# The first tiles of a fused retention and gated feed-forward kernel are re-ordered, and two more chunks are transposed by DMA

## The chip, the cores and the metric

The kernel runs on one NeuronCore of one Trainium2 chip. The metric is device time in microseconds, the lower the better. Median before: 242.88 us over nine runs (242.76 to 243.0).

## What is computed

The reference is a retention layer followed by a gated feed-forward layer:

```
gamma[h] = 1 - 2**(-5-h);  scale = 1/sqrt(64)
for t in range(768):                       # for each of 4 batches, 8 heads
    state = gamma*state + outer(k[t], v[t])
    y[t]  = scale * q[t] @ state
x   = y, heads side by side                # 3072 tokens x 512
out = (sigmoid(x @ w_gate) * (x @ w_val)) @ w_out    # 512 -> 1536 -> 512
```

All inputs and the output are float32 in device memory. There are 3072 tokens.

## The kernel before

**Chunks and tiles.** The recurrence is computed in 24 chunks of 128 tokens, six to a batch; chunk `g` is chunk `g % 6` of batch `g // 6`. Four chunks make a token tile of 512, and there are six tiles. Attention for a chunk has these steps, each a small function:

- `transposes` (L134): eight TensorE transposes of k and q, copied from PSUM by ScalarE (L140). For chunks `g >= XBAR` (12), `xbar` (L142) does it with two DMA transposes on SP's queue instead.
- `scale_v` (L148): v times a decay table `tabv`, on VectorE for chunks below 8 and on GpSimd from there on.
- `scores` (L153): eight products k.q into two PSUM banks; `masks` (L162): two VectorE multiplications with the causal mask.
- `inter` (L168): four products of the running state `zbd` with q; `state` (L175): eight products k.v that are added to the state in PSUM; `state_out` (L185): two ScalarE copies of it into `zbd`.
- `intra` (L192): eight products of the masked scores with v; `y_out` (L199): VectorE multiplies the result with a decay table `taby` into `xT`, the feed-forward's input, already transposed.

**Feed-forward.** `up(t, n1)` (L235) makes one of 12 blocks of 128 hidden columns: four matmuls with `wg` and four with `wv` into two PSUM banks, a Sigmoid on ScalarE (L246), a product on VectorE (L247). The pool `pf` has three such banks. `down(t, sm)` (L249) makes 128 of the tile's output rows with twelve matmuls, a ScalarE copy into one of three `ob` buffers (L255) and a store on SP's queue (L257).

**Order.** The schedule is written by hand: each engine runs its instructions in the order of the program. The first three chunks are done before any feed-forward work (L275 to L319), with Identity products (`keep_on`, L259) placed between the steps on TensorE. The fourth chunk is mixed with the first four ups, which take 384 columns at first and 128 more when the fourth chunk is there (L332). From then on, tile `t`'s loop (L336) places the nine attention steps of tile `t + 1` evenly between its 12 ups and 4 downs; in tile 0 they begin after the seventh group.

**Queues.** GpSimd's queue issues nearly all loads, in program order: chunks 1 to 3, weights, chunks 4 to 7; then, when tile `t` begins, the loads of tile `t + 2`'s chunks, and after them the four `scale_v` of tile `t + 1`'s chunks, where these are GpSimd's. So chunk 8's scaling stands behind the loads of chunks 12 to 15. A load on this queue also waits until the load eight places before it has landed, since eight semaphores are used in turn. SP's queue holds the stores and the DMA transposes: those for chunks 12 to 15 stand between tile 0's four stores and tile 1's.

The functions that the diff touches:

Of the kernel before, what the change touches and what calls it, by code (L numbers as in the profile page):

```python
# [17 lines left out]
def kernel(  # L18
# [31 lines left out]

    NG = B * NCH
    NT = N_TOK // 512
    XBAR = 12
    qn, kn, vf = {}, {}, {}

    def src(x, g):
        b, c = divmod(g, NCH)
        return x[b, :, c * C:(c + 1) * C, :].rearrange("h s d -> s h d")
# [11 lines left out]
    def load_chunk(g):  # L70
        load_kq(g)
        load_v(g, nc.gpsimd)
# [16 lines left out]
    kf = const.tile([C, H, D], F32, name="kf")  # L89
    qf = const.tile([C, H, D], F32, name="qf")  # L90
    nc.sync.dma_start(out=kf, in_=src(k, 0))
    nc.scalar.dma_start(out=qf, in_=src(q, 0))
    load_v(0, nc.sync)
    tokv = const.tile([128, NCH], I32, name="tokv")
    nc.gpsimd.iota(tokv, pattern=[[C, NCH]], base=0, channel_multiplier=1)
    ident = const.tile([128, 128], BF16, name="ident")
    make_identity(nc, ident)
    toky = const.tile([128, S], I32, name="toky")
    nc.gpsimd.iota(toky, pattern=[[1, S]], base=0, channel_multiplier=0)
    load_chunk(1)  # L100
    causal = const.tile([128, 128], F32, name="causal")
    nc.gpsimd.memset(causal, 1.0)
# [10 lines left out]
    for p in range(NP):  # L113
        nc.vector.memset(lgp[0:D, p:p + 1], lg[2 * p])
        nc.vector.memset(lgp[D:128, p:p + 1], lg[2 * p + 1])
    zbd = [const.tile([128, NP, C], BF16, name=f"zbd{i}") for i in range(2)]
    for t in zbd:
        nc.vector.memset(t, 0.0)
# [2 lines left out]
    def make_taby(cols):  # L121
        for p in range(NP):
            nc.scalar.activation(taby[:, p, cols], toky[:, cols], AX.Exp, scale=lgp[:, p:p + 1], bias=lsc)  # L123

    causal4 = causal.unsqueeze(1).to_broadcast([128, NP, 128])

# [7 lines left out]
    def transposes(g):  # L134
        tp = pa.tile([128, 2 * NP, C], BF16, tag="tp", name="tp")
        for i, x in enumerate((kn[g], qn[g])):
            for p in range(NP):
                nc.tensor.transpose(tp[:, i * NP + p, :], pair(x, p), ident)  # L138
        qkT[g] = at.tile([128, 2 * NP, C], BF16, tag="qkT", name="qkT", bufs=3)
        nc.scalar.activation(qkT[g], tp, AX.Copy)  # L140
# [7 lines left out]
    def scale_v(g, eng):  # L148
        vs[g] = ld.tile([C, H, D], BF16, tag="vs", name="vs", bufs=4)
        eng.tensor_tensor(vs[g], vf[g], tabv[:, g % NCH, :].unsqueeze(2).to_broadcast([C, H, D]),  # L150
                          op=ALU.mult)

    def scores(g):  # L153
        t = qkT[g]
        sc[g] = (pa.tile([128, NP, C], F32, tag="sA", name="sA"),
                 pa.tile([128, NP, C], F32, tag="sB", name="sB"))
        for p in range(NP):
            for i in range(2):
                half = slice(i * D, (i + 1) * D)
                nc.tensor.matmul(sc[g][i][:, p, :], t[half, p, :], t[half, NP + p, :], start=True, stop=True)  # L160

    def masks(g):  # L162
        stA[g] = at.tile([128, NP, C], BF16, tag="stA", name="stA")
        stB[g] = at.tile([128, NP, C], BF16, tag="stB", name="stB")
        nc.vector.tensor_tensor(stA[g], sc[g][0], causal4, op=ALU.mult)  # L165
        nc.vector.tensor_tensor(stB[g], sc[g][1], causal4, op=ALU.mult)  # L166

    def inter(g):  # L168
        y[g] = pa.tile([128, NP, C], F32, tag="y", name="y")
        if g % NCH > 0:  # L170
            for p in range(NP):
                nc.tensor.matmul(y[g][:, p, :], zbd[(g - 1) % 2][:, p, :], qkT[g][:, NP + p, :],  # L172
                                 start=(p == 0), stop=False, skip_group_check=True)

    def state(g):  # L175
        b, c = divmod(g, NCH)
        if c == 0:
            zps[b] = pa.tile([128, NP, D], F32, tag="z", name="z", padded_shape=[128, NP, C])
        if c < NCH - 1:
            for p in range(NP):  # L180
                for i in range(2):
                    nc.tensor.matmul(zps[b][i * D:(i + 1) * D, p, :], kn[g][:, 2 * p + i, :], vs[g][:, 2 * p + i, :],  # L182
                                     start=(c == 0 and p == 0), stop=True, skip_group_check=True)
# [8 lines left out]
    def intra(g):  # L192
        first = g % NCH == 0
        for p in range(NP):
            for i, st in enumerate((stA[g], stB[g])):
                nc.tensor.matmul(y[g][i * D:(i + 1) * D, p, :], vs[g][:, 2 * p + i, :], st[:, p, :],  # L196
                                 start=(first and p == 0), stop=True, skip_group_check=True)

    def y_out(g):  # L199
        c = g % NCH  # L200
        if g % 4 == 0:
            xT[g // 4] = at.tile([128, NP, 512], BF16, tag="xT", name="xT")
        col = (g % 4) * C
        nc.vector.tensor_tensor(xT[g // 4][:, :, col:col + C], y[g], taby[:, :, c * C:(c + 1) * C], op=ALU.mult)  # L204
# [21 lines left out]
    def attention(t):  # L226
        g = 4 * t
        return [lambda: step_t(g), lambda: step_s(g), lambda: step_t(g + 1), lambda: step_y(g, g + 1),
                lambda: step_t(g + 2), lambda: step_y(g + 1, g + 2), lambda: step_t(g + 3),
                lambda: step_y(g + 2, g + 3), lambda: step_y(g + 3)]  # L230
# [39 lines left out]
    for s in range(4):  # L270
        load_out(s)
    for g in range(5, 8):
        load_chunk(g)

    kn[0] = ld.tile([C, H, D], BF16, tag="kn", name="kn")  # L275
    qn[0] = ld.tile([C, H, D], BF16, tag="qn", name="qn")
    make_taby(slice(0, 256))
    nc.vector.tensor_copy(kn[0], kf)
    nc.scalar.copy(qn[0], qf)
    keep_on(36)  # L280
    transposes(0)
    keep_on(8)
    scale_v(0, nc.vector)
    scores(0)
    state(0)
    state_out(0)
    masks(0)
    keep_on(8)
    make_taby(slice(256, 384))
    transposes(1)  # L290
    scale_v(1, nc.vector)
    inter(0)
    intra(0)
    y_out(0)
    keep_on(10)
    scores(1)
    state(1)
    state_out(1)
    masks(1)
    inter(1)  # L300
    keep_on(10)
    make_taby(slice(384, 512))
    transposes(2)
    intra(1)
    scale_v(2, nc.vector)
    y_out(1)
    keep_on(12)
    scores(2)
    state(2)
    state_out(2)  # L310
    masks(2)
    inter(2)
    keep_on(12)
    make_taby(slice(512, 768))
    nc.scalar.preload_act_table(AX.Sigmoid)  # L315
    intra(2)
    y_out(2)
    scale_v(3, nc.vector)
    keep_on(8)  # L319
    up(0, 0, 0, 384)  # L320
    transposes(3)
    up(0, 1, 0, 384)
    scores(3)
    masks(3)
    inter(3)
# [3 lines left out]
    intra(3)  # L329
    y_out(3)  # L330
    up(0, 3, 0, 384)
    for n1 in range(4):  # L332
        up(0, n1, 384, 512)


    for t in range(NT):  # L336
        groups = [lambda n1=n1: up(t, n1) for n1 in range(0 if t else 4, NFF)]
        groups += [lambda sm=sm: down(t, sm) for sm in range(4)]
        steps = attention(t + 1) if t + 1 < NT else []
        if t + 2 < NT:  # L340
            for g in range(4 * t + 8, 4 * t + 12):
                load_chunk(g)
        first = 0 if t else 6
        done = 0
        for i, group in enumerate(groups):
            if i == len(groups) - 5:
                for g in range(4 * t + 8, 4 * t + 12):
                    if XBAR <= g < NG:
                        xbar(g)
            group()  # L350
            upto = -(-len(steps) * (i + 1 - first) // (len(groups) - first))
            while done < min(upto, len(steps)):
                steps[done]()
                done += 1


# [28 lines left out]
```

## Time and profile before

| | |
|---|---|
| median of nine runs | 242.88 us |
| the profiled execution: device time | 242.81 us |
| its span, first to last instruction | 241.1 us |
| granted TensorE clock | 1.000 |
| TensorE busy | 228.5 us, 95% of the span |
| VectorE, ScalarE, GpSimd busy | 101.4, 95.0, 91.5 us |
| first up begins / tile 1's first up begins | 19.0 / 62.2 us |
| DMA transposes | 24, median 9.3 us to landing |

Busy times are per engine and overlap. A line of the timeline has start, duration, engine, line of the kernel, operation, output and inputs, and in brackets how long the engine had been idle and what ended that. A line of the waits has who waited for whom, then microseconds in total, times, and the longest. "DMA to landing" is from the issue of a load to its arrival.

### The profile page before, as it was taken

The page shows a single profiled execution, that of the slowest core. Times are in us where ns is not written, and L with a number is a line of the kernel's source. Part 1 is how long each engine was busy: PE and PEld are TensorE (multiplying, and loading weights), DVE is VectorE, ACT ScalarE, POOL GpSimd, SP SyncE. Part 2 cuts the span into 40 slices and gives each one's busy share as a digit, 9 for nine tenths or more (in the row PEclk, how much of TensorE's full clock was granted, in tenths as well). Part 3 has the DMA queues.
Part 4 walks back from the last instruction along what each step waited for, and adds up shares of the span by engine and source line. Part 5 has one row for each costly group of instructions (what it writes and reads, how often), then busy time and mean ns, then how long its engine had stood idle before and what let it go on. Part 6 is the DMA issues. An engine that isn't in the chain of part 4 may idle for free.

```text
span 241.1 us, 4300 instructions
## 1 busy us (share of the span) xinstructions
PE 228.5 (95%) x1720; PEld 117.8 (49%) x1720; DVE 101.4 (42%) x168; ACT 95.0 (39%) x179; POOL 91.5 (38%) x111
## 2 busy tenths in 40 slices
PE   6689998998899999999999999999999999999993
PEld 6565644554445554444554445444445554444441
DVE  2565534474256623256632255642256641243300
ACT  7778434343544432334333324232233431333221
POOL 8996574887899252996101101111000000000000
PEclk9999999999999999999999999999999999999999
DMA  9999999999999999999992363002200012100022
GB/s 148 180 199 197 195 209 205 180 198 229 230 184 106 124 126 111 264 158 151 148 95 87 109 91 67 0 15 82 81 3 0 0 46 82 48 3 0 0 87 87
DMA packets 77267, 27.27 MB, mean 113 GB/s; under 512 B 65024, under 2 KB 72704, under 8 KB 77248
## 3 DMA queue, kind: packets, MB, share of 16 engines
q0 software_dynamic: 57616, 16.78, 76.8%
q1 hardware_dynamic: 18592, 9.97, 21.1%
q10 hardware_dynamic: 1040, 0.26, 0.5%
q8 instruction: 13, 0.21, 0.4%
q14 instruction: 6, 0.05, 0.1%
HBM read 28.31 MB, written 6.29 MB: 144 GB/s over the span
## 4 chain that ended last, share of the span: by engine, by line
PE 89%; ACT 9%; issue 1%; DVE 0%; ACTq 0%
PE ff L242 51%; PE ff L252 26%; PE sA L160 3%; ACT taby L123 3%; ACT qkT L140 3%; PE y L196 2%; PE z L182 2%; PE y L172 2%; PE tp L138 2%; ACT zbd L190 1%; ACT L315 1%; ACT L109 1%; ACT ob L255 0%; ACT tabv L109 0%; ACT gs L246 0%
## 5 line engine op out<-in xcount | busy, mean ns | idle before, releaser
L247 DVE TENSOR_TENSOR hT<-gs,ff 128x512 bf16<-128x512 f32 (+2 forms) x76 | 50.0, 660 | 80.3 <-PE ff L242 76.6
L242 PE MATMUL ff<-xT,wg 128*128 128x512 bf16 (+2 forms) x304 | 74.7, 368 | 1.2 <-DVE xT L204 1.1
L242 PE MATMUL ff<-xT,wv 128*128 128x512 bf16 (+2 forms) x304 | 74.6, 368 | 0.0
L246 ACT ACTIVATE gs<-ff 128x512 f32<-128x512 f32 (+2 forms) x76 | 43.7, 574 | 69.3 <-PE ff L242 69.3
L252 PE MATMUL ff<-wo,hT 128*128 128x512 bf16 x288 | 65.0, 379 | 0.0
L242 PEld LDWEIGHTS <-wv 128*128 128x128 bf16 x304 | 29.3, 98 | 33.2
L242 PEld LDWEIGHTS <-wg 128*128 128x128 bf16 x304 | 27.9, 98 | 31.3 <-issue 1.4
L252 PEld LDWEIGHTS <-hT 128*128 128x128 bf16 x288 | 27.3, 98 | 32.1
L255 ACT COPY ob<-ff 128x512 f32<-128x512 f32 x24 | 14.1, 586 | 55.0 <-PE ff L252 50.7
L150 POOL TENSOR_TENSOR vs<-vf,tabv 128x512 bf16<-128x512 f32 x16 | 16.5, 1045 | 48.0 <-PE y L196 43.0
L62 POOL DMA_DIRECT2D vf<-in_v_dram x23 | 20.7, 900 | 15.7 <-DMA kn<-in_k_dram 10.6
L204 DVE TENSOR_TENSOR xT<-y,taby 128x512 bf16<-128x512 f32 x24 | 16.4, 683 | 20.6 <-PE y L196 20.6
L165 DVE TENSOR_TENSOR stA<-sA,causal 128x512 bf16<-128x512 f32 x24 | 16.5, 687 | 19.9 <-PE sB L160 19.9
L67 POOL DMA_DIRECT2D kn<-in_k_dram x23 | 20.7, 902 | 5.1 <-DMA qn<-in_q_dram 2.1
L68 POOL DMA_DIRECT2D qn<-in_q_dram x23 | 20.4, 887 | 4.2 <-DMA wo<-in_moe_w_out_dram 2.2
L190 ACT CAST zbd<-z 64x256 bf16<-64x256 f32 x40 | 14.7, 367 | 12.2 <-PE z L182 11.9
L166 DVE TENSOR_TENSOR stB<-sB,causal 128x512 bf16<-128x512 f32 x24 | 16.3, 680 | 0.0
L140 ACT ACTIVATE qkT<-tp 128x1024 bf16<-128x1024 bf16 x12 | 12.3, 1023 | 4.8 <-PE tp L138 4.8
L262 PE MATMUL ff<-ident 128*128 128x128 bf16 x104 | 9.0, 252 | 1.6 <-POOL ident masks.py:199 1.6
L160 PE MATMUL sA<-qkT 64*128 64x128 bf16 x48 | 4.7, 219 | 5.5 <-ACT qkT L140 5.4
L196 PE MATMUL y<-stA,vs 128*64 128x128 bf16 x96 | 9.9, 222 | 0.0
L196 PE MATMUL y<-stB,vs 128*64 128x128 bf16 x96 | 9.5, 221 | 0.0
(40 smaller groups left out, 107.1 us busy)
## 6 DMA issues: line engine op xcount, KB each, us to landing
out_dram<-ob SPq DMA_DIRECT2D x24, 256.0 KB, 2.0
vf<-in_v_dram POOLq DMA_DIRECT2D x23, 256.0 KB, 8.5
kn<-in_k_dram POOLq DMA_DIRECT2D x23, 128.0 KB, 8.6
qn<-in_q_dram POOLq DMA_DIRECT2D x23, 128.0 KB, 10.2
wg<-in_moe_w_gate_dram POOLq DMA_DIRECT2D x6, 256.0 KB, 8.8
wv<-in_moe_w_val_dram POOLq DMA_DIRECT2D x6, 256.0 KB, 9.3
wo<-in_moe_w_out_dram POOLq DMA_DIRECT2D x4, 384.0 KB, 10.2
qf<-in_q_dram ACTq DMA_DIRECT2D x1, 256.0 KB, 4.6
```

Of the source, the lines that this page charges most:

```text
L62: eng.dma_start(out=vf[g], in_=src(v, g))
L67: nc.gpsimd.dma_start(out=kn[g], in_=src(k, g))
L68: nc.gpsimd.dma_start(out=qn[g], in_=src(q, g))
L140: nc.scalar.activation(qkT[g], tp, AX.Copy)
L150: eng.tensor_tensor(vs[g], vf[g], tabv[:, g % NCH, :].unsqueeze(2).to_broadcast([C, H, D]), op=ALU.mult)
L165: nc.vector.tensor_tensor(stA[g], sc[g][0], causal4, op=ALU.mult)
L190: nc.scalar.copy(zbd[g % 2][half, :, half], zps[b][half])
L196: nc.tensor.matmul(y[g][i * D:(i + 1) * D, p, :], vs[g][:, 2 * p + i, :], st[:, p, :], start=(first and p == 0), stop=True, skip_group_che ...
L242: nc.tensor.matmul(u[:, lo:hi], w[:, kk, n1 * 128:(n1 + 1) * 128], xT[t][:, kk, lo:hi], start=(kk == 0), stop=(kk == KT - 1))
L246: nc.scalar.activation(gs[:, lo:hi], ps[0][:, lo:hi], AX.Sigmoid)
L247: nc.vector.tensor_tensor(hT[t][:, n1, lo:hi], gs[:, lo:hi], ps[1][:, lo:hi], op=ALU.mult)
L252: nc.tensor.matmul(o, hT[t][:, n1, sm * 128:(sm + 1) * 128], wo[:, n1, :], start=(n1 == 0), stop=(n1 == NFF - 1))
```

## The change

- v of chunks 0 and 1 is scaled on GpSimd, between its loads, instead of on VectorE.
- The decay table `taby` is computed on ScalarE for 384 columns only; GpSimd makes the other 384 from them with one multiplication (`extend_taby`). The loads of the last three pairs of weight blocks, of chunk 4 and later stand behind it.
- The load of q for chunk 0 goes from ScalarE's queue to SP's; ScalarE's first table is loaded ahead of time, the Sigmoid table after chunk 2's transposes are copied.
- The steps of chunks 0 to 3 are in another order with fewer Identity products; chunk 3's transposes come after two ups instead of one.
- The last 128 columns of the first four ups go into one pair of PSUM banks (`up_columns`).
- `down` is cut into halves of six matmuls, and steps are placed by a list of group numbers. Chunk 7's last step goes behind tile 1's first up, which takes 384 columns.
- `XBAR` is 10: chunks 10 and 11 are transposed by DMA, placed on SP's queue when tile 1's third group begins, ahead of those for chunks 12 to 15.

```diff
-    XBAR = 12
+    XBAR = 10
...
-    nc.scalar.dma_start(out=qf, in_=src(q, 0))
+    nc.sync.dma_start(out=qf, in_=src(q, 0))
+    nc.scalar.preload_act_table(AX.Exp)
...
+    def extend_taby():
+        nc.gpsimd.tensor_tensor(taby[:, :, 384:768], taby[:, :, 0:384],
+                                gup.unsqueeze(2).to_broadcast([128, NP, 384]), op=ALU.mult)
...
+    def up_columns(t, n1s, lo, hi):
+        n = hi - lo
+        ps = []
+        for w in (wg, wv):
+            u = pf.tile([128, 512], F32, tag="ff", name="ff")
+            for i, n1 in enumerate(n1s):
+                for kk in range(KT):
+                    nc.tensor.matmul(u[:, i * n:(i + 1) * n], w[:, kk, n1 * 128:(n1 + 1) * 128], xT[t][:, kk, lo:hi],
+                                     start=(kk == 0), stop=(kk == KT - 1))
+            ps.append(u[:, :len(n1s) * n])
+        gs = ffn.tile([128, 512], F32, tag="gs", name="gs")
+        g = gs[:, :len(n1s) * n]
+        nc.scalar.activation(g, ps[0], AX.Sigmoid)
+        nc.vector.tensor_tensor(hT[t][:, n1s[0]:n1s[-1] + 1, lo:hi], g.rearrange("p (i n) -> p i n", n=n),
+                                ps[1].rearrange("p (i n) -> p i n", n=n), op=ALU.mult)
...
-    def down(t, sm):
-        o = pf.tile([128, 512], F32, tag="ff", name="ff")
-        for n1 in range(NFF):
+    def down(t, sm, part):
+        if part == 0:
+            po[0] = pf.tile([128, 512], F32, tag="ff", name="ff")
+        o = po[0]
+        half = NFF // 2
+        for n1 in range(part * half, (part + 1) * half):
...
+        if part == 0:
+            return
...
+    scale_v(0, nc.gpsimd)
     load_gate_val(0)
+    scale_v(1, nc.gpsimd)
     load_chunk(3)
-    for s in range(1, NFF // 2):
+    load_gate_val(1)
+    load_gate_val(2)
+    make_taby(slice(0, 256))
...
+    keep_on(36)
+    transposes(0)
+    make_taby(slice(256, 384))
+    extend_taby()
+    for s in range(3, NFF // 2):
         load_gate_val(s)
     load_chunk(4)
...
-    for n1 in range(4):
-        up(0, n1, 384, 512)
+    up_columns(0, range(4), 384, 512)
...
     for t in range(NT):
+        groups, steps, place = ups(t) + downs(t), [], []
+        if t == 0:
+            groups = groups[4:]
+            steps = [lambda: step_t(4), lambda: step_s(4), lambda: step_y(4), lambda: step_t(5), lambda: step_s(5),
+                     lambda: step_t(6), lambda: step_y(5, 6), lambda: step_t(7), lambda: step_y(6, 7)]
+            place = [4, 5, 7, 9, 10, 11, 12, 13, 14]
+        elif t + 1 < NT:
+            steps = attention(t + 1)
+            place = [0, 1, 3, 5, 7, 8, 10, 13, 17]
+        if t == 1:
+            groups[:2] = [lambda: up(1, 0, 0, 384), lambda: step_y(7), lambda: up(1, 1, 0, 384),
+                          lambda: up_columns(1, range(2), 384, 512)]
+            place = [p + 2 for p in place]
...
         for i, group in enumerate(groups):
+            if t == 1 and i == 2:
+                for g in range(XBAR, 12):
+                    xbar(g)
+            if i == len(groups) - 9 and t > 0:
+                for g in range(4 * t + 8, min(4 * t + 12, NG)):
+                    xbar(g)
             group()
+            for p, step in zip(place, steps):
+                if p == i:
+                    step()
```

The order of the steps of chunks 0 to 3 on TensorE, before and after (T transposes, S scores, Z state, I inter, A intra, K and a number for Identity products, U for an up):

```
before: K36 T0 K8 S0 Z0 K8 T1 A0 K10 S1 Z1 I1 K10 T2 A1 K12 S2 Z2 I2 K12 A2 K8 U0 T3 U1 S3 I3 Z3 U2 A3 U3
after:  K36 T0 K8 S0 K8 T1 Z0 A0 K8 S1 K4 I1 Z1 T2 A1 K12 S2 I2 Z2 K10 A2 K8 U0 U1 T3 S3 I3 Z3 U2 A3 U3
```

More of the change, by code (lines that the diff above doesn't have):

```diff
@@ L97 @@
     make_identity(nc, ident)
-    toky = const.tile([128, S], I32, name="toky")
-    nc.gpsimd.iota(toky, pattern=[[1, S]], base=0, channel_multiplier=0)
+    toky = const.tile([128, 384], I32, name="toky")
+    nc.gpsimd.iota(toky, pattern=[[1, 384]], base=0, channel_multiplier=0)
     load_chunk(1)
@@ L115 @@
         nc.vector.memset(lgp[D:128, p:p + 1], lg[2 * p + 1])
+    gup = const.tile([128, NP], F32, name="gup")
+    for h in range(H):
+        nc.vector.memset(gup[h % 2 * D:(h % 2 + 1) * D, h // 2:h // 2 + 1], math.exp(384 * lg[h]))
     zbd = [const.tile([128, NP, C], BF16, name=f"zbd{i}") for i in range(2)]
@@ L247, in up @@
         nc.vector.tensor_tensor(hT[t][:, n1, lo:hi], gs[:, lo:hi], ps[1][:, lo:hi], op=ALU.mult)
-    def down(t, sm):
-        o = pf.tile([128, 512], F32, tag="ff", name="ff")
-        for n1 in range(NFF):
+    def up_columns(t, n1s, lo, hi):
[13 more added lines that the diff above has]
+                                ps[1].rearrange("p (i n) -> p i n", n=n), op=ALU.mult)
+    po = {}
+    def down(t, sm, part):
[4 more added lines that the diff above has]
+        for n1 in range(part * half, (part + 1) * half):
             nc.tensor.matmul(o, hT[t][:, n1, sm * 128:(sm + 1) * 128], wo[:, n1, :],
                              start=(n1 == 0), stop=(n1 == NFF - 1))
+        if part == 0:
+            return
         ob = ffn.tile([128, D_MODEL], F32, tag="ob", name="ob")
@@ L262, in keep_on @@
             nc.tensor.matmul(u[:, :128], ident, ident, start=True, stop=True)
+    scale_v(0, nc.gpsimd)
     load_gate_val(0)
+    scale_v(1, nc.gpsimd)
     load_chunk(3)
-    for s in range(1, NFF // 2):
+    load_gate_val(1)
+    load_gate_val(2)
+    make_taby(slice(0, 256))
+    kn[0] = ld.tile([C, H, D], BF16, tag="kn", name="kn")
+    qn[0] = ld.tile([C, H, D], BF16, tag="qn", name="qn")
+    nc.vector.tensor_copy(kn[0], kf)
+    nc.scalar.copy(qn[0], qf)
+    keep_on(36)
[3 more added lines that the diff above has]
+    for s in range(3, NFF // 2):
         load_gate_val(s)
@@ L273 @@
         load_chunk(g)
[L275 to L281, printed above, removed]
     keep_on(8)
-    scale_v(0, nc.vector)
     scores(0)
+    masks(0)
+    keep_on(8)
+    transposes(1)
+    inter(0)
     state(0)
     state_out(0)
[L287 to L292, printed above, removed]
     intra(0)
     y_out(0)
-    keep_on(10)
+    keep_on(8)
     scores(1)
+    masks(1)
+    keep_on(4)
+    inter(1)
     state(1)
     state_out(1)
[L299 to L302, printed above, removed]
     transposes(2)
+    nc.scalar.preload_act_table(AX.Sigmoid)
     intra(1)
+    y_out(1)
     scale_v(2, nc.vector)
-    y_out(1)
     keep_on(12)
     scores(2)
+    masks(2)
+    inter(2)
     state(2)
     state_out(2)
[L311 to L315, printed above, removed]
+    keep_on(10)
     intra(2)
@@ L320 @@
     up(0, 0, 0, 384)
+    up(0, 1, 0, 384)
     transposes(3)
-    up(0, 1, 0, 384)
     scores(3)
@@ L331, with ups, downs @@
     up(0, 3, 0, 384)
-    for n1 in range(4):
-        up(0, n1, 384, 512)
-    for t in range(NT):
-        groups = [lambda n1=n1: up(t, n1) for n1 in range(0 if t else 4, NFF)]
-        groups += [lambda sm=sm: down(t, sm) for sm in range(4)]
-        steps = attention(t + 1) if t + 1 < NT else []
+    up_columns(0, range(4), 384, 512)
+    def ups(t):
+        return [lambda n1=n1: up(t, n1) for n1 in range(NFF)]
+    def downs(t):
+        return [lambda sm=sm, i=i: down(t, sm, i) for sm in range(4) for i in range(2)]
+    for t in range(NT):
+        groups, steps, place = ups(t) + downs(t), [], []
[11 more added lines that the diff above has]
+            place = [p + 2 for p in place]
         if t + 2 < NT:
@@ L342 @@
                 load_chunk(g)
-        first = 0 if t else 6
-        done = 0
         for i, group in enumerate(groups):
[L346 to L349, printed above, removed]
+            if t == 1 and i == 2:
[4 more added lines that the diff above has]
+                    xbar(g)
             group()
[L351 to L354, printed above, removed]
+            for p, step in zip(place, steps):
+                if p == i:
+                    step()
 _INS = ['q', 'k', 'v', 'moe_w_gate', 'moe_w_val', 'moe_w_out']
```

## The prediction

> **What bounds the kernel now.** I read the page first, then TensorE's waits, its timeline, the chain of waits, and at last GpSimd's timeline with the DMA landings. All times are of the profiled execution: span 241.1, device time 242.81, so 1.7 lies around the span; the median of the nine runs is 0.07 above it.
>
> ```profile
> PE 228.5 (95%) x1720; PEld 117.8 (49%) x1720; DVE 101.4 (42%) x168; ACT 95.0 (39%) x179; POOL 91.5 (38%) x111
> ```
>
> TensorE is the bound, but only in part of the span. Its waits between 62 and 237 us are one line, so from there on the order of its work is its time. What idles, idles earlier:
>
> ```profile
> PE ff L242 <- DVE xT L204: 0.8, 1, 0.8
> ```
>
> ```profile
> 19.03 0.81 PE L242 MATMUL ff<-xT,wg 128*128 128x384 bf16 x4 [0.30 <-DVE xT L204]
> ...
> 42.48 0.23 PE L160 MATMUL sA<-qkT 64*128 64x128 bf16 x1 [1.12 <-ACT qkT L140]
> ...
> 57.13 0.23 PE L160 MATMUL sA<-qkT 64*128 64x128 bf16 x1 [1.18 <-ACT qkT L140]
> ```
>
> The first up starts at 19.03, and twice later scores wait for ScalarE's copy of the transposes that stand right before them. The chain of waits says why 19 us pass: between the copies ScalarE computes decay tables.
>
> ```profile
> 10.73 1.03 ACT qkT L140
> ...
> 13.28 1.65 ACT taby L123 x4
> 14.95 1.03 ACT qkT L140
> ```
>
> There is a second line of supply, silent in the waits because it is just in time. GpSimd issues all loads and, in the same order, scales v from chunk 8 on:
>
> ```profile
> 68.45 0.89 POOL L62 DMA_DIRECT2D vf<-in_v_dram  x1 [0.51 <-DVE stB L166]
> 69.35 4.04 POOL L150 TENSOR_TENSOR vs<-vf,tabv 128x512 bf16<-128x512 f32 x4
> ```
>
> ```profile
> 74.51 0.32 PE L182 MATMUL z<-vs,kn 128*64 128x64 bf16 x8
> ```
>
> The scaling of chunk 8 begins only when the last load of chunk 15 is issued, ends at 70.4, and TensorE's first reader, the state of chunk 8, comes at 74.5. The slack is 4.1 us. GpSimd is not busy there, it is paced: by the order of waits each load waits until the load eight places earlier has landed. The last load of chunk 15 waits for the k of chunk 13 (issued 60.09):
>
> ```profile
> DMA to landing us min/median/max: 7.8/7.8/7.8
> ```
>
> It lands at 67.9, and the issue follows at 68.45. The page's DMA row is at 9 up to about 130 us.
>
> **What the Trainium skill says.** "DMA: Bandwidth & Descriptors", Queues, rings and completion order: each DMA engine takes turns between the queues that have work, packet by packet. The trace agrees: once SP's transposes are in flight, GpSimd's loads slow down (below). "GPSIMD Engine Reference", 3.1 Elementwise: two-input work takes about 2.6 cycles an element; the trace has 1045 ns for 512 columns, 2.0 ns each, close to it. "TensorE: Matmul & The Clock Gate", What's actually happening: after an idle window of about 3.4 us the array runs at half rate until about 3.4 us of work have passed. The trace shows the cold rate at the start alone (36 Identity products in 3.97 us, 0.11 each, later twelve in 0.84); no stall in it is long enough to test the rest.
>
> **The change, part by part.**
>
> *Start.* The query load leaves ScalarE's queue and the table load starts about 0.5 us earlier; the tables for columns 384 to 768 leave ScalarE (1.65 + 2.07) for one GpSimd multiply. ScalarE's second copy can then start at 9.1 instead of 10.73 (first copy until 7.4, one table set of 1.65). The v scaling on GpSimd stands behind chunk 2's loads (end 8.4 now, 8.0 with the shorter counter): 8.0 to 9.1 for chunk 0, then two weight issues of 0.78, chunk 1 at 10.7 to 11.7. The state of chunk 1 needs that, then 0.24 state, the copy to zbd 0.76, chunk 2's transposed copy 1.03 to 13.8; scores, masks (0.63 and 0.68), intra, product to xT (0.69) follow as now (16.03 to 19.03, 3.0). First up at about 16.8: minus 2.2. The Identity products are fewer, but beside waits either way: nothing. The eight memsets of the new factor (0.06 each) lie in VectorE's 2.37 of waiting for k, and the Sigmoid table (1.28) goes from the first up's own eviction to 13.8 to 15.1, where only chunk 2's zbd stands behind it, wanted after 20: nothing.
>
> *Loads behind it.* GpSimd works 1.05 twice, and the table multiply: 1536 columns at 2.0 ns, 3.1 us (1.5 if it ran at VectorE's 0.69 per 512 and a bit under; 4.5 if slowed). The queue had 5 to 10 us of loads in flight there (weights land 5.0 to 11.0 after issue), so most hides; I take the load stream 0.5 us later (0 to 2).
>
> *Tile 0.* From the first up to the end of tile 1's second up, TensorE's own work is 12 + 2 ups of 1.73, 4 downs of 2.59, chunks 3 to 7 at 1.1 to 1.4: 40.9 us; before it takes 46.8 (19.0 to 65.8, without chunk 8's transposes). Half downs and hand placement put 1.3 to 1.7 us of work behind each transpose, more than the copy's 1.03; one wait remains, chunk 3's scores right behind its transposes, 1.1. So 42.5 rather than 46.8: minus 4.3. Tile 1's first up takes 384 columns, so that chunk 7's last product (end 61.4 now, then 0.70 and a wait of 0.79) lies behind it. The bank shared by four column groups replaces eight evictions by two and is in this. The chunks 5 to 7 land about when wanted (chunk 7's k at 48.9); half a us here or there.
>
> *Transposes.* Chunks 10 and 11 go from TensorE to SP's DMA queue: minus 2 x 0.45 = 0.9 on TensorE; plus four DMA transposes. They stand on SP behind tile 0's four stores, which come about 5 us earlier than now, and wait for the k of chunk 10 (lands 58.4 now), so they start about 59, ahead of the eight that start at 64.77 now.
>
> Were that all: 242.8 - 2.2 - 4.3 - 0.9 = 235.4. It is not, for the second line of supply does not move with it. After tile 1's second up (16.8 + 42.5 = 59.3) come four ups (6.9), two transposes, two scores and an inter (1.6): TensorE wants chunk 8's v at 67.8. GpSimd's order there is as before; with loads 0.5 later v is there at 70.9. And now the four transposes come in front of just the load that GpSimd waits for. Their price from the trace:
>
> ```profile
> L145 SPq DMA_TRANSPOSE qkX<-kn x4: 1190/1272/1428, 64.8 to 81.0; - x4
> L145 SPq DMA_TRANSPOSE qkX<-qn x4: 1188/1275/2083, 66.2 to 83.0; - x4
> ```
>
> From chunk 7's k (48.9) to chunk 13's (67.9) 18 loads land in 19.0 us, 1.05 each. Chunk 15's k is the sixth after that one and takes 14.8 from its issue at 66.19, landing at 81.0: 13.1 us for six, 6.8 above pace, while four transposes land: 1.7 each. In the later batch, from chunk 20's k (105.9) to chunk 23's v (125.2), 11 loads take 19.3 with eight transposes: 1.0 each. The transposes issued from 59 start to hold loads up some 4 us later (as those of 64.77 did from 69), when five loads are still to land up to chunk 13's k. I take four transposes at 1.5, the same stretch weighing more: 6.0; bounds three at 1.0 (3.0) and six at 1.7 (10.2). So that k lands at 67.9 + 0.5 + 6.0 = 74.4, the last load of chunk 15 is issued from 75.0 to 75.9, chunk 8's v is scaled at 77.0.
>
> **The sum.** The state of chunk 8 moves from 74.5 to 77.0: plus 2.5. It stands behind the same work in both orders, and after it the order is the same but for 0.9 of transposes: minus 0.9. The stall, 67.8 to 77.0, is over the idle window: half rate for 3.4 us costs an estimated 1.7 (0 to 3.4), by the skill's clock page. Together plus 3.3: 246.1. So all of tile 0's gain is spent in one wait.
>
> **Rivals.**
> *The transposes hold the loads less (faster).* With none, the state is at 71.0, minus 3.5, minus 0.9, a stall of 3.2 with no cold clock: 238.4. It turns at 3.5 + 0.9 - 1.7 = 2.7 us of delay, two transposes at 1.4. For it: the first six loads after 64.77 landed at pace. Against: the store before those transposes landed at 67.1 and held them in their queue; the new ones have none in front.
> *A second wall (slower still).* Four more transposes go ahead of tile 1's first store on SP. It is issued at 90.78 now and lands 8.9 later, just when the fourth copy needs its buffer (99.78). With both at upper bounds, v at 81 and 2 us of this: 251.
> *No such wait:* 235.4, if chunk 8's v comes earlier than GpSimd's order allows; nothing speaks for it.
> *Gain and wait cancel:* within 0.2%, the least this kernel's measurement tells from no change.
>
> **Numbers.** The forecast 0.50; second wall 0.20; faster 0.23; no wait 0.02; cancel 0.05. Faster 0.25, same 0.05, slower 0.70. The range runs from the faster rival's better half to the second wall's nearer part: 240.0 to 250.0.
>
> **What would show it.** Right: first up near 17, tile 1 begun near 55, then one TensorE wait of 6 to 10 us at the state of chunk 8, ended by GpSimd's vs; chunk 13's k landing at 72 or later; a cold clock after it. Wrong: vs ready before 72, or no wait there; then the faster rivals hold. A wait at tile 1's fourth copy shows the second wall.

## The result, and the profile after

| | before | changed |
|---|---|---|
| median | 242.93 us (31 runs) | 247.14 us (10 runs) |
| lowest to highest | 242.75 to 243.12 | 245.96 to 248.55 |
| span of the profiled execution | 241.1 us | 245.4 us |
| granted TensorE clock in it | 1.000 | 0.986 |
| first up begins | 19.0 us | 16.9 us |
| tile 1's first up begins | 62.2 us | 56.8 us |
| state of chunk 8 begins | 74.5 us | 77.5 us |

The change makes the kernel slower: the ratio is 1.0179 (95% interval 1.0165 to 1.0194), 4.2 us. In this and all later ratios, executions more than 1.5% above the fastest of the same kernel are left out; medians and ranges take in every one.

The page of the changed kernel, its busy row, the rows of TensorE and its clock over forty slices of 6.1 us each, and the chain that ended last by engine:

```profile
PE 230.1 (94%) x1710; PEld 118.4 (48%) x1710; DVE 102.1 (42%) x172; ACT 88.8 (36%) x167; POOL 95.9 (39%) x114
...
PE   7898999999943999999999999999999999999993
...
PEclk9999999999996899999999999999999999999999
...
PE 63%; DMA 21%; POOL 11%; issue 2%; ACT 1%; DVE 0%; POOLq 0%; ACTq 0%
```

TensorE's busy share fell by one point only. What tells is where it idles: one hole, in the twelfth and thirteenth slices (67 to 80 us), and right after it the clock is down. The chain of work that ended last, 89% TensorE before, now goes through DMA and GpSimd for a third. Bounded by TensorE's order before, the first third of this kernel is now bounded by its supply.

TensorE's waits name the hole (total, times, longest):

```profile
PE z L190 <- POOL vs L158: 7.1, 1, 7.1
```

This line is not in the waits of the kernel before at all. TensorE's timeline of the changed kernel, at the first up and around the hole:

```profile
16.88 0.81 PE L250 MATMUL ff<-xT,wg 128*128 128x384 bf16 x4 [0.30 <-DVE xT L212]
...
70.14 0.22 PE L168 MATMUL sB<-qkT 64*128 64x128 bf16 x1
77.48 0.42 PE L190 MATMUL z<-vs,kn 128*64 128x64 bf16 x8 [7.12 <-POOL vs L158]
...
78.26 1.89 PE L250 MATMUL ff<-xT,wg 128*128 128x512 bf16 x4
79.94 1.91 PE L250 MATMUL ff<-xT,wv 128*128 128x512 bf16 x4
81.65 1.29 PE L250 MATMUL ff<-xT,wg 128*128 128x512 bf16 x4
82.78 1.03 PE L250 MATMUL ff<-xT,wv 128*128 128x512 bf16 x4
```

TensorE is 4.2 us ahead of the kernel before when it comes to the state of chunk 8 (70.3 against 74.5) and 3.0 behind when it leaves (77.5). The next three groups of matmuls show 1.89, 1.91 and 1.29 us where the fourth shows 1.03, the usual.

GpSimd's timeline answers to the two GpSimd lines shown of before:

```profile
61.65 0.88 POOL L67 DMA_DIRECT2D kn<-in_k_dram  x1
...
75.47 0.89 POOL L62 DMA_DIRECT2D vf<-in_v_dram  x1 [2.17 <-DMA kn<-in_k_dram]
76.37 4.04 POOL L158 TENSOR_TENSOR vs<-vf,tabv 128x512 bf16<-128x512 f32 x4
```

The last load of chunk 15 (75.47) was held by "DMA kn": that is chunk 13's k, issued at 61.65. The view of that one load:

```profile
DMA to landing us min/median/max: 13.3/13.3/13.3
```

Before it took 7.8. It now lands at 74.9, and the issue follows 0.6 later. It is the last of several late loads: chunk 15's k (70.88) and q (72.43) had been held in the same way by chunk 12's q and v, which took 11.4 and 11.1. With chunk 13's k alone in time, this issue could have come earlier only by the 2.2 us that its line shows as idle. SP's timeline of the changed kernel shows what is new beside it:

```profile
59.95 1.29 SPq L153 DMA_TRANSPOSE qkX<-kn  x1
61.36 1.23 SPq L153 DMA_TRANSPOSE qkX<-qn  x1
63.42 1.25 SPq L153 DMA_TRANSPOSE qkX<-kn  x1
64.76 1.39 SPq L153 DMA_TRANSPOSE qkX<-qn  x1
```

These are the transposes of chunks 10 and 11. The first stands 1.7 us ahead of that load, where before it the first of all stood at 64.77, 4.7 us behind.

### The profile page after: what moved, and what is told of

It reads as the page before. It is cut to its first block, busy times and chain, and to the rows that moved or that the text cites. A ratio compares the mean times of both kernels' runs of the same rounds, so it can differ in the third digit from the quotient of the medians.

```text
span 245.4 us, 4283 instructions
## 1 busy us (share of the span) xinstructions
PE 230.1 (94%) x1710; PEld 118.4 (48%) x1710; DVE 102.1 (42%) x172; ACT 88.8 (36%) x167; POOL 95.9 (39%) x114
## 4 chain that ended last, share of the span: by engine, by line
PE 63%; DMA 21%; POOL 11%; issue 2%; ACT 1%; DVE 0%; POOLq 0%; ACTq 0%
PE ff L250 39%; PE ff L281 18%; DMA kn<-in_k_dram 9%; DMA wo<-in_moe_w_out_dram 5%; DMA out_dram<-ob 4%; DMA wg<-in_moe_w_gate_dram 3%; POOL vf L62 2%; PE sA L168 2%; PE y L204 2%; POOL wg L81 2%; POOL wv L81 1%; POOL kn L67 1%; POOL qn L68 1%; PE z L190 1%; POOL vs L158 1%
## 5 line engine op out<-in xcount | busy, mean ns | idle before, releaser
L255 DVE TENSOR_TENSOR hT<-gs,ff 128x512 bf16<-128x512 f32 (+1 forms) x72 | 48.6, 676 | 77.3 <-PE ff L250 71.5
L250 PE MATMUL ff<-xT,wg 128*128 128x512 bf16 (+1 forms) x288 | 73.9, 380 | 0.4 <-DVE xT L212 0.3
L250 PE MATMUL ff<-xT,wv 128*128 128x512 bf16 (+1 forms) x288 | 73.5, 378 | 0.0
L254 ACT ACTIVATE gs<-ff 128x512 f32<-128x512 f32 (+1 forms) x72 | 42.3, 588 | 72.4 <-PE ff L250 72.3
L250 PEld LDWEIGHTS <-wv 128*128 128x128 bf16 x288 | 28.4, 99 | 33.3 <-issue 1.1
L250 PEld LDWEIGHTS <-wg 128*128 128x128 bf16 x288 | 27.0, 99 | 31.8 <-issue 2.7
L158 POOL TENSOR_TENSOR vs<-vf,tabv 128x512 bf16<-128x512 f32 x18 | 18.5, 1048 | 43.7 <-PE y L204 38.8
L198 ACT CAST zbd<-z 64x256 bf16<-64x256 f32 x40 | 14.7, 366 | 20.0 <-PE z L190 19.6
L190 PE MATMUL z<-vs,kn 128*64 128x64 bf16 x160 | 6.4, 203 | 7.3 <-POOL vs L158 7.1
L148 ACT ACTIVATE qkT<-tp 128x1024 bf16<-128x1024 bf16 x10 | 10.3, 1025 | 3.4 <-PE tp L146 3.4
## 6 DMA issues: line engine op xcount, KB each, us to landing
qn<-in_q_dram POOLq DMA_DIRECT2D x23, 128.0 KB, 11.4
```

Of the source, the lines that this page charges most:

```text
L250: nc.tensor.matmul(u[:, lo:hi], w[:, kk, n1 * 128:(n1 + 1) * 128], xT[t][:, kk, lo:hi], start=(kk == 0), stop=(kk == KT - 1))
```

## The experiments

Each starts from the changed kernel unless it says otherwise, and none leaves out a step of the computation. "The first wall" is the wait at chunk 8's state, "the second wall" one at tile 1's fourth output copy.

### 1. The transposes back where they were

```diff
-    XBAR = 10
+    XBAR = 12
```

> The changed kernel with XBAR back at 12: chunks 10 and 11 are transposed on TensorE again, all else stays. My theory (the four extra DMA transposes delay chunk 13's k, and through GpSimd's order chunk 8's v): that load lands at 69 to 70 instead of 74.9, v is ready at about 72 instead of 77.4, the wait at chunk 8's state is 1 to 2 us, no cold clock; 247.1 - 5.5 - 2.1 + 0.9 = 240.5. Rival (the re-ordering of tile 0 itself makes GpSimd late): v comes at 76 or later and the time stays at 246 or above.

Measured: 240.04 us (239.94 to 240.34), ratio to before 0.9879 (0.9864 to 0.9894). First the view of chunk 13's k, then the waits, both of this run:

```profile
DMA to landing us min/median/max: 7.4/7.4/7.4
```

```profile
PE z L190 <- POOL vs L158: 0.9, 2, 0.7
```

That k was issued at 61.7, as in the changed kernel, and lands 5.8 us earlier; the hole is 0.7 and the clock 0.998. So putting chunks 10 and 11 back on TensorE takes away the whole loss, and all the rest of the change is a gain of 2.9 us: the state of chunk 8 comes at 71.73, 2.8 before its time in the kernel before.

### 2. Only the transposes, in the kernel before

The same two chunks are transposed by DMA in the kernel before, behind tile 0's stores.

```diff
-    XBAR = 12
+    XBAR = 10
...
+            if t == 1 and i == 0:
+                for g in range(XBAR, 12):
+                    xbar(g)
-            if i == len(groups) - 5:
+            if i == len(groups) - 5 and t > 0:
```

> The kernel before with XBAR = 10 alone, the transposes of chunks 10 and 11 put behind tile 0's stores. My theory: here they begin only after the last of these stores (about 62), TensorE wants chunk 8's v at 74.5 and it comes at about 74, so hardly a wait there; minus 0.9 of TensorE work, but tile 1's first store is pushed back and the fourth copy waits for it, 0 to 2.5 us: 242 to 244.5, 243.3 as one number. Rival (four more DMA transposes cost what they cost in the changed kernel, wherever TensorE stands): 246 or more.

Measured: 243.59 us (241.97 to 248.87, 9 runs), ratio 1.0023 (0.9987 to 1.0059): no difference that can be told, but a spread that the kernel before has not. Its first transpose was issued at 61.66, for the stores of tile 0 come later here. Chunk 13's k was issued at 60.21, ahead of it, and landed after 8.1. So alone the edit did not bring the first wall. Its profiled execution was the longest of the nine (248.87) and had the second wall instead (4.7 us of TensorE).

### 3. Chunk 8's v away from GpSimd

```diff
-        scale_v(g, nc.vector if g < 8 else nc.gpsimd)
+        scale_v(g, nc.vector if g < 12 else nc.gpsimd)
```

> The changed kernel with v of chunks 8 to 11 scaled on VectorE, so that nothing of tile 1 stands behind GpSimd's loads. My theory: the wait of 7.1 us and the cold clock after it go, but TensorE then runs into the second wall, the fourth output copy of tile 1, which waits for a store behind twelve DMA transposes: about 6 us and a cold clock again; 244 to 247. Rival (one wall only): 247.1 - 7.1 - 2.1 = 238.

Measured: 246.94 us (244.7 to 250.91), ratio 1.013 (1.006 to 1.02). VectorE's v does not stand behind the loads in GpSimd's order, and the first wall is gone. The time is hardly better. TensorE's waits in the profiled execution (the longest of the four), then ScalarE's and SP's timeline and a line of the chain of waits:

```profile
PE ff L250 <- ACT ob L286: 11.8, 1, 11.8
```

```profile
85.13 0.59 ACT L286 COPY ob<-ff 128x512 f32<-128x512 f32 x1 [2.86 <-PE ff L281]
...
107.60 0.59 ACT L286 COPY ob<-ff 128x512 f32<-128x512 f32 x1 [15.57 <-DMA out_dram<-ob]
```

```profile
93.16 1.19 SPq L153 DMA_TRANSPOSE qkX<-kn  x1
94.44 1.29 SPq L153 DMA_TRANSPOSE qkX<-qn  x1
95.82 1.74 SPq L288 DMA_DIRECT2D out_dram<-ob  x3
```

```profile
70.46 22.68 DMA kn<-in_k_dram
```

The first output rows are in their buffer at 85.7. Their store stands in SP's program behind the last of twelve transposes, and these two, chunk 15's, stood still until its k had landed: issued at 70.46, it took 22.7 us, to 93.14. So the second wall too comes from a late load, by way of SP. The store lands at 107.5, and only then is a buffer free for the fourth copy. In the changed kernel the first wall covered this second one, since it let TensorE come 9 us later to the end of tile 1.

### 4. The same, with chunks 10 and 11 on TensorE

Edit 3 and edit 1 together.

> The changed kernel with XBAR at 12 and v of chunks 8 to 11 scaled on VectorE. My theory: what is left of the wait for GpSimd's v (0.9 us in the kernel with XBAR 12 alone) goes, and the stores of tile 1 are not behind twelve transposes: 239.2. Rival (the stores still make a wait once TensorE is ahead): 241 or more.

Measured: 238.72 us (238.69 to 239.2), ratio 0.9831 (0.9816 to 0.9846). With neither wall, the first tiles are worth 4.2 us.

### 5. The stores on another queue

Edit 3, and tile 1's stores issued by ScalarE, so that no transpose stands ahead of them.

```diff
-        nc.sync.dma_start(out=out[row:row + 128, :], in_=ob)
+        (nc.scalar if t == 1 else nc.sync).dma_start(out=out[row:row + 128, :], in_=ob)
```

> The changed kernel (XBAR 10) with v of chunks 8 to 11 on VectorE and the four stores of tile 1 issued by ScalarE instead of SP, so that they don't stand behind the twelve DMA transposes. My theory: the second wall is the order on SP's queue; both walls go: 238. Rival (the DMA engines are too full whichever queue the stores take): a wait of some us at tile 1's fourth copy stays, 242 or more.

Measured: 259.53 us (255.78 to 266.1), ratio 1.06 (1.05 to 1.07), far from both. The waits of this run:

```profile
ACT ob L286 <- DMA qkX<-qn: 10.1, 2, 5.9
ACT zbd L198 <- DMA qkX<-qn: 9.8, 1, 9.8
ACT gs L254 <- DMA qkX<-qn: 5.0, 1, 5.0
```

ScalarE waits for transposes with which it has nothing to do. In this program the DMAs that SP and ScalarE issue share eight semaphores, and each waits until the last user of its semaphore has landed. Each of the four stores came to one that a transpose had used (they were issued at 95.07, 100.57, 107.06 and 112.65, each within 0.1 us of such a landing), and the waiting issue stood in ScalarE's own order, ahead of evictions and Sigmoids. The edit put in a wait of its own and tells nothing of the two theories.

### 6. Two chunks' transposes behind the stores

The second wall again, without another queue: edit 3, and chunks 14 and 15 are transposed behind tile 1's stores. (In the expectation, "Ten chunk transposes..." is a slip for the eight transposes named right behind it.)

```diff
-                for g in range(4 * t + 8, min(4 * t + 12, NG)):
+                for g in range(4 * t + 8, min(4 * t + (10 if t == 1 else 12), NG)):
                     xbar(g)
...
+        if t == 1:
+            xbar(14)
+            xbar(15)
```

> The changed kernel with the v of chunks 8 to 11 scaled on VectorE, and the DMA transposes of chunks 14 and 15 put on SP behind tile 1's four stores instead of ahead of them; no step is left out. Ten chunk transposes... eight DMA transposes then stand ahead of the first store, as in the kernel before, and not twelve. Theory (with the v of chunk 8 off GpSimd, what is left of the loss is the second wall: the first store of tile 1 stands behind twelve transposes on SP and the fourth output copy waits for it): the wait of 11.8 us of TensorE on ScalarE's output copy goes, and the time is 238.0, what the same edit gave with transposes from chunk 12 on (238.72) less 0.9 for two chunks off TensorE. Rival (the store is held by the traffic of loads and transposes as such, wherever SP issues it): the store still lands 10 us or more after its issue, the wait stays at 4 us or more, and the time is 242 or above.

Measured: 238.65 us (237.55 to 244.99), ratio 0.979 (0.9773 to 0.9807). SP's timeline:

```profile
86.17 9.95 SPq L288 DMA_DIRECT2D out_dram<-ob  x4
```

The first store is issued 0.6 after its copy began, not 10.7, and no copy of tile 1 waits. Chunk 13's k took 14.7 us here, longer than in the changed kernel, and it cost nothing, since nobody waited for it. So the two walls are the loss, and each comes from a place in a queue. A wait of 1.0 us of TensorE turns up one tile later, at tile 2's fourth copy.

### 7. Is it the number of transposes? One chunk instead of two

After these runs I held that each transpose in flight costs the loads a fixed 1.5 us.

```diff
-    XBAR = 10
+    XBAR = 11
```

> The changed kernel with XBAR 11: two extra DMA transposes instead of four, the first when chunk 11's k has landed (about 63.5 instead of 60). My theory: the delay of chunk 13's k comes to some 2 us, chunk 8's v at about 74, a wait of 3 us and a short cold clock: 242.5, between the 240.0 of XBAR 12 and the 247.1 of XBAR 10. Rival (a threshold in SP's queue, not a price per transpose): either 240 or 247.

Measured: 239.6 us (239.18 to 240.02), ratio 0.9862 (0.9845 to 0.9879). My theory falls: half of the transposes did that load no harm at all (chunk 14's k, issued 1.4 behind the first, took 11.8 against 7.6 in run 1, and nobody waited long for it), and the run is 0.44 faster than with none. SP's timeline, and the view of chunk 13's k:

```profile
63.13 1.31 SPq L153 DMA_TRANSPOSE qkX<-kn  x1
```

```profile
L67 POOL DMA_DIRECT2D kn<-in_k_dram x1: 893/893/893, 61.5 to 61.5; - x1
...
DMA to landing us min/median/max: 7.0/7.0/7.0
```

Without chunk 10's, the first transpose waits for chunk 11's k and is issued at 63.13, behind the load that matters. The same reading over all fourteen kernels of this study, those of the runs below too (times of issue in us, then from issue to landing):

| kernel | first transpose of this stretch | chunk 13's k | landed after |
|---|---|---|---|
| before | 64.77 | 60.09 | 7.8 |
| 1 (from chunk 12 on) | 66.19 | 61.68 | 7.4 |
| 4 (from chunk 12 on) | 66.12 | 61.61 | 7.4 |
| 11 (from chunk 12 on) | 66.53 | 61.75 | 7.9 |
| 8 (SP's order) | 66.40 | 61.43 | 7.9 |
| 9 (SP's order) | 67.14 | 62.62 | 7.4 |
| 7 (from chunk 11 on) | 63.13 | 61.48 | 7.0 |
| 2 (in the kernel before) | 61.66 | 60.21 | 8.1 |
| 12 (from chunk 11 on) | 62.24 | 60.93 | 8.9 |
| 5 (stores on ScalarE) | 60.12 | 61.82 | 12.0 |
| changed | 59.95 | 61.65 | 13.3 |
| 6 (two chunks behind) | 59.62 | 61.33 | 14.7 |
| 10 (Identity products) | 60.31 | 62.02 | 14.9 |
| 3 (v on VectorE) | 60.13 | 61.84 | 15.8 |

That load is in time or nearly so wherever it is issued 1.3 us or more ahead of the first transpose. It is late in the five kernels where it is issued 1.7 us behind it, and there it stands behind two transposes; no run puts it behind one.

The border is soft, and the order of issue alone is no rule for every load. Chunk 13's q, issued 0.6 ahead in run 2, took 12.8; chunk 12's k, 1.9 ahead in the changed kernel, took 9.4; but chunk 14's v, 0.5 behind in run 1, took 8.2, and there the k and v of chunk 15, 1.4 and 3.5 behind, took 10.9 and 13.0. The DMA records of the traces fit this: the packets of the transposes (256 bytes each) first move 1.8 to 4.4 us after the first issue. That is 4.1 to 8.4 us after the issue of chunk 13's k in the nine kernels where it is in time or nearly so, and 2.1 to 2.7 us after it in the five where it is late.

### 8. The same transposes in another order

To part order from number, all twelve stay, and chunk 12's go ahead of those of chunks 10 and 11.

```diff
-                for g in range(XBAR, 12):
+                for g in (12, 10, 11):
                     xbar(g)
...
-                for g in range(4 * t + 8, min(4 * t + 12, NG)):
+                for g in range(13 if t == 1 else 4 * t + 8, min(4 * t + 12, NG)):
```

> The changed kernel with the same twenty-eight DMA transposes, only in another order on SP: those of chunk 12 go ahead of those of chunks 10 and 11, so that the first one waits for chunk 12's k (about 66) and is issued after chunk 13's k (about 61.6), not before it. No step is left out. Theory (a load is late when it is issued after the first transpose, whatever the number of transposes): chunk 13's k lands 7 to 8 us after its issue, at about 69, chunk 8's v is there at about 71.5, the first wall is gone; twelve transposes still stand ahead of tile 1's first store and TensorE comes there earlier, so the second wall takes its place with a wait of 4 to 12 us at the fourth output copy: 244 (241 to 248). Rival (each transpose costs the loads a fixed time, so that twelve before tile 1's end hold chunk 8's v as before): a wait at chunk 8's state of 5 us or more, 246 to 247.

Measured: 243.61 us (241.56 to 247.5), ratio 0.9949 (0.9929 to 0.9969). TensorE's timeline in the profiled execution (245.98):

```profile
71.91 0.32 PE L190 MATMUL z<-vs,kn 128*64 128x64 bf16 x8 [1.02 <-POOL vs L158]
...
81.92 0.26 PE L168 MATMUL sA<-qkX 64*128 64x128 bf16 x1 [3.96 <-DMA qkX<-qn]
```

The cause is confirmed: with the same number of transposes, all issued later than that load, chunk 13's k lands after 7.9 us, and the first wall is 1.0. The time is near what the theory gave, but not from the wall that it named. Chunk 10's transposes are late themselves now: its q, issued at 71.78, lands at 81.88, and TensorE wants its scores at 78.0. No copy waits.

### 9. The same order, and two chunks behind the stores

Edit 8, with edit 6's change of SP's queue.

> The kernel of the run before, with the transposes of chunks 14 and 15 put on SP behind tile 1's four stores as well. All operations of the changed kernel are there, only SP's order differs, and no step is left out. Theory (the whole loss comes from where the transposes stand on SP: ahead of chunk 13's k, and ahead of tile 1's stores): no wait of over 1 us at chunk 8's state or at tile 1's output copies, 239.2: what transposes from chunk 11 on gave (239.6) less 0.45 for one more chunk off TensorE. Rival (the number of transposes matters too, so that the loads or stores are late in another place): a TensorE wait of over 2 us on GpSimd's v or on an output copy, 241.5 or above.

Measured: 246.56 us (242.84 to 247.86, 11 runs), ratio 1.0055 (1.0018 to 1.0091), which is that of the fastest four; the other seven lie at 246.5 or above, some 1.5% over the kernel before. The theory of 239.2 falls, and the rival is the nearer one. The profiled execution (243.18) has 2.2 us at chunk 8's state, with chunk 13's k landing 7.4 after its issue but issued 1.0 later than in the changed kernel, and 1.6 for chunk 10's transposes. With v on GpSimd no order that was tried is free: ahead of the loads the transposes hold up v, behind them they are late themselves. Why most runs of this version are longer than the profiled one isn't settled.

### 10. The clock alone

Identity products (110) in front of chunk 8's state, so that TensorE does not idle.

```diff
+        if g == 8:
+            keep_on(110)
```

> The changed kernel with 110 Identity products (6.2 us at the full clock) in front of chunk 8's state, so that TensorE is not idle while v is missing. My theory: v comes as late as before, but the clock stays at full rate: minus 2.1 us, 245.0. Rival (the half rate after the wait is not caused by the idling): no change, 247.

Measured: 250.29 us (245.03 to 254.11, 4 runs): inconclusive. Chunk 13's k landed at 76.9 in the profiled execution, which was the longest, so that the stall outlasted the products; it also had 3.9 us of the second wall. Its timeline:

```profile
70.41 6.31 PE L295 MATMUL ff<-ident 128*128 128x128 bf16 x110
79.51 0.32 PE L190 MATMUL z<-vs,kn 128*64 128x64 bf16 x8 [2.79 <-POOL vs L158]
...
79.99 1.50 PE L252 MATMUL ff<-xT,wg 128*128 128x512 bf16 x4
81.28 1.91 PE L252 MATMUL ff<-xT,wv 128*128 128x512 bf16 x4
82.99 1.45 PE L252 MATMUL ff<-xT,wg 128*128 128x512 bf16 x4
```

The waits for transfers vary by more than the effect. The one run whose clock stayed at 1.000 took 245.03, what the theory gave, but that is one run.

### 11 and 12. A version that beats both

Two edits on run 4: chunk 3's transposes go ahead of the second up again, which takes away the 1.1 us of scores waiting for their copy; then, on top of that, `XBAR` 11.

```diff
+    transposes(3)
     up(0, 1, 0, 384)
-    transposes(3)
```

> As the kernel with XBAR 12 and v of chunks 8 to 11 on VectorE, and chunk 3's transposes before the second up instead of behind it, so that this up covers ScalarE's copy. My theory: the wait of 1.1 us at chunk 3's scores goes, 238.3. Rival (TensorE is held by the loads behind it): no change against the same kernel without the swap.

> The best version so far (v of chunks 8 to 11 on VectorE, chunk 3's transposes ahead of the second up) with DMA transposes from chunk 11 on instead of 12; no step is left out. Theory (two more transposes cost nothing where they start behind the loads that matter, and take 0.45 us from TensorE): 238.0, no wait on GpSimd or on the output copy at chunk 8 and at tile 1's end. Rival (two more transposes ahead of tile 1's stores bring a part of the second wall): a wait of 1 us or more at tile 1's fourth output copy, 239.5 or above.

Measured: 238.48 us (238.1 to 238.89), ratio 0.9822 (0.9806 to 0.9838), and 238.26 (237.47 to 243.83), ratio 0.9814 (0.978 to 0.9848). The wait of 1.1 went, and of it 0.24 in the time, which the spreads don't tell from none. `XBAR` 11 shows 2.1 us of the second wall in its profiled execution (240.4), as its rival said, and spreads. I would keep the first of the two: 4.5 us below the kernel before, 8.7 below the changed one, and steady.

## Why the prediction was right, step by step

- *What bounds it.* Right: the tile's gain ran into the second line of supply, at the place and through the chain that was named. Run 1 shows it by taking the transposes away, run 3 by taking the v off GpSimd.
- *Start.* First up at 16.88, predicted 16.8. The table multiply took 2.83 us, 3.1 was taken (the lower bound of 1.5 was a slip: 0.69 for 512 columns makes 2.1 for 1536).
- *Load stream, +0.5.* Mis-sized, within its bounds: in run 1, without the early transposes, chunk 13's k lands at 69.12 against 67.88 before, +1.2.
- *Tile 0, minus 4.3.* Mis-sized by more than half. From the first up to the end of tile 1's second one it takes 43.3 us (16.88 to 60.16), predicted 42.5, but both ups of tile 1 still lack their last 128 columns there. A fair stretch runs from the first up until TensorE stands at chunk 8's state: 53.5 us (16.88 to 70.36) against 55.5 before (19.03 to 74.51), a gain of 2.0 where the prediction's times give 4.5. TensorE is busy for 52.0 and 52.1 us of it, so nearly all of the gain is waiting that went: of 3.1 us before (1.12, 1.18 and 0.79) 1.4 are left, the predicted 1.1 and 0.3 at chunk 8's scores. The 40.9 us of own work was too low a sum: up to 60.16 TensorE is busy for 42.1, with 0.9 of those two ups still to come.
- *When TensorE wants the v.* Wrong: 70.3, not 67.8. Of the 2.5, 0.9 is from the start of tile 1 (59.3 against 60.16), 0.9 is the last 128 columns of tile 1's two ups (sixteen matmuls, 60.61 to 61.5), which I left out, 0.3 a wait at scores, the rest is in the rounded pieces. All of it lies inside the stall, so the wait is 7.1 and not 9.2 and the total did not suffer. That is luck: without walls the prediction's 235.4 would have been missed, since run 6, without either wall and with both chunks off TensorE, took 238.65 (237.55 at the least).
- *The four transposes, 6.0.* Chunk 13's k landed at 74.9 (predicted 74.4), 5.8 later than in run 1. That the size was right is partly luck, for the price per transpose behind it does not hold: in run 7 two transposes cost that load nothing, and in run 8 twelve, all issued behind it, cost it nothing either. What counts is how early the first one is issued. The prediction's other remark, that transposes hold up loads only some 4 us after their issue, does hold (their packets start after 1.8 to 4.4 us). The skill's "DMA: Bandwidth & Descriptors", Queues, rings and completion order, on the taking of turns, is in line with the loads of one queue slowing under the other's transposes, but does not give the size.
- *Chunk 8's v.* Scaled from 76.37 to 77.44, predicted 77.0; the state +2.97, predicted +2.5.
- *Cold clock, 1.7.* Mis-sized. The views of windows have, for three stretches after the stall, the span, the busy times by engine and then the mean clock (0.50, 0.59, 1.00):

```profile
77.40:78.30 0.90, 0.82 (x17) 0.65 (x17) 0.00 (x0) 0.36 (x1) 0.90 (x2) 0.50 1.99 151
78.30:83.00 4.70, 4.70 (x15) 1.75 (x15) 1.38 (x2) 0.99 (x4) 4.70 (x6) 0.59 1.92 114
83.00:90.00 7.00, 7.00 (x57) 3.52 (x56) 3.85 (x6) 3.10 (x6) 3.14 (x5) 1.00 2.23 112
```

  From 78.26 to 82.78 TensorE did what takes 2.6 us at full clock (three groups 0.86 apart), 1.9 more; the state and intra before it took 0.78 where run 1 has 0.47. That is 2.2, predicted 1.7 (0 to 3.4). The half rate lasted for 4.7 us of work (77.48 to 82.18), not for the 3.4 that the estimate took.
- *Minus 0.9 on TensorE.* Not seen by itself in the changed kernel; run 7 against run 1 gives 0.44 for one chunk, run 6 against run 4 between 0.07 (medians) and 1.0 us (ratios) for two, with too few runs to tell.
- *Second wall.* Named as a rival, there but small. ScalarE's timeline of the changed kernel:

```profile
105.15 0.59 ACT L286 COPY ob<-ff 128x512 f32<-128x512 f32 x1 [3.78 <-DMA out_dram<-ob]
```

  The copy waits 3.8 us, TensorE 0.2 (105.57 to 105.78). I had it as the slower end of the first wall; run 3 shows that the first covers it: it grows to 11.8 when the first is gone.
- *The sum.* 2.97 + 2.2 - 0.9 + 0.2 = 4.5 against 4.3 between the spans and 4.2 between the medians; predicted 3.3. The missing 0.9 is 0.5 of the state, 0.5 of the clock, 0.2 of the second wall, less the 0.3 by which my sum of the measured pieces is over.
- *The rivals.* "The transposes hold the loads less" asked for under 2.7 us of delay; it was 5.8. One reason given against it was wrong: the new transposes did have a store in front of them. Tile 0's last one was issued at 57.35 and landed at 63.9, and their packets start at 64.0. "No such wait" is out by the 7.1.

Open are two things: why all versions with two more chunks on DMA vary by 2.6 to 10 us from run to run, where the kernel before varies by 0.4, and what the cold clock costs in the total (run 10 did not show it).

## What to carry to other kernels

When one line of work is made faster, look for the lines that feed it without a wait in the profile, and compute their slack (here 4.1 us): any gain beyond it turns into a wait, and anything that delays the feeding line eats the slack from the other side. A transfer that is added to another queue is not free because the queue was idle: ask which load is issued right behind it and who waits for that one, and which store stands behind it in its own queue. Two walls in a row are tested together, since the first one hides the second.

## What was not expected of the hardware

- DMA transposes slow the loads of another queue, and by how much depends on how early the first is issued: 7.0 to 8.9 us to landing for chunk 13's k where it is issued 1.3 us or more ahead of it, 12.0 to 15.8 where it is issued 1.7 behind (fourteen kernels, the table above), with loads in between that fit neither.
- The clock changes in steps that do not begin with the wait. In run 10 TensorE was idle for 2.8 us, then worked 0.9 us at the full clock before the clock halved, from 80.42 to 83.83, 3.41 us. In the changed kernel it was half from 75.36 to 82.18, 6.83 us. The skill's "TensorE: Matmul & The Clock Gate", What's actually happening, speaks of an idle window of about 3.4 us that runs freely; these steps of 3.41 and 6.83 us agree. But the window need not be wholly idle: the one that ends at 80.42, if it is as long, holds 0.9 us of work.
- A DMA issued by ScalarE waited for transposes issued by SP (run 5), 4.2 to 9.8 us each, through a semaphore that they share in this program: that is its order of waits, not the transfer itself.
